# One tile's transpose moved from TensorE to the DMA engines, in an attention and FFN kernel whose TensorE order is a fixed list

## The chip, the cores and the metric

One core of one Trainium2 chip. The time is the device time of one launch in microseconds, as the median of several runs; "span" is the profiled execution from its first to its last instruction, about 1.7 us less. All positions are us from the start of the span. In the profile's lines PE is TensorE, PEld its weight loads, DVE VectorE, ACT ScalarE, POOL GpSimd and SP SyncE; SPq and ACTq are the instruction queues of SP and ACT, and L383 is line 383 of the kernel.

## The reference, cut to what matters

```python
# q, k, v: (4 batches, 8 heads, 768, 64); window 128 and 4 sink keys
scores = scale * q @ k.T                       # per head
a = softmax(where(sink | in_window, scores, -1e9))
x = (a @ v)  -> (4*768, 512)                   # heads side by side
out = ((x @ w1) * (x @ w2)) @ w3 @ w_out       # (3072, 512) float32
```

## The kernel before: the parts that matter

The kernel folds w3 and w_out into one matrix while the inputs load, then works through the batches. Of each batch b and each tile t of 256 rows: `sc` (scores of one pair of heads), exponential on ScalarE, mask multiply on VectorE, `av` (weighted values, then the division into `xn`), the transpose of `xn` into `xT`, gates `g` (x @ w1 copied by ScalarE, x @ w2 multiplied onto it by VectorE), and projections `p`. A task of TensorE's list is named after its kind and its place: `sc`, `av` and `xt` by batch, pair of heads and tile, `g` by batch, half of the rows, column block and which of the two matrices, `p` by batch and block of 128 rows. The transpose is done in one of two ways, by the list `X_XPOSE`:

```python
def x_transposes(b, r0, t):                    # on TensorE, through PSUM
    me = ("xt", b, r0, t)
    xt = ps_mm.tile([P, 2, 2, P], BF16, tag="mm", name="xt")
    for r in range(2):
        for i in range(2):
            nc.tensor.transpose(xt[:, r, i, :], xns[b, t][:, i, r0 + r, :, :]..., ident[:])
    yield
    copy_on(me, xT[b][:, r0:r0 + 2, t * 256:(t + 1) * 256], xt[:]...)
    yield

def x_transposes_dma(b, t, i):                 # 128 rows x 512, by DMA, issued on SP
    q0 = t * 256 + i * P
    nc.sync.dma_start_transpose(out=xT[b][:, :, q0:q0 + P], in_=xns[b, t][:, i]...)
    yield
```

The exponential and its multiply, whose buffers will matter (the pool's default is three):

```python
work = ctx.enter_context(tc.tile_pool(name="work", bufs=3))
...
ex = work.tile([P, 2, 512], BF16, tag="ex", name="ex")
nc.scalar.activation(ex[:, :, c0:], sc[:, :, c0:], ACTF.Exp, scale=scale)
yield
am = work.tile([P, 2, 512], BF16, tag="am", bufs=4, name="am")
nc.vector.tensor_mul(am[:, :, c0:], ex[:, :, c0:], mk)
```

TensorE's order is a list in the source (`PLAN`), found by a search. While the program is built, a small model of the engines runs through it and puts the instructions of ScalarE, VectorE and SP in the order in which they become ready by its own clock. It knows the landings (`arrive`, `LATER`), the latencies of DMA transposes (`XP_US`, `XX_US`), and, of the rings of buffers, these two in PSUM; a few buffers in SBUF it knows as dependencies (those of `xn`, for one), but the ring of `ex` not:

```python
rings = {n: [[0.0] for _ in range(k)] for n, k in (("mm", 4), ("sc", 2))}
...
queue[e].append((at + HOP, YIELD.get(k["name"][0], 0.1), us, k))
```

The softmax here doesn't subtract the row's maximum and nothing guards it: scores larger than these inputs give would overflow.

## Time and profile before

| | before |
|---|---|
| median of the runs | 196.68 us (4 runs, 196.50 to 196.72) |
| profiled span | 195.0 us |
| TensorE starts its unbroken work | 11.1 us |
| last TensorE piece starts | 190.16 us |
| x tiles transposed on TensorE / by DMA | 6 / 6 |

The profile's own lines are shown in the prediction. What to take from them: a chain made of TensorE alone, piece on piece, means that the time is a sum of TensorE's work. A change can then only save what it takes out of that sum, and can lose any amount by a wait.

### The profile page before, as it was taken

To read this page: it belongs to the slowest core of one execution; us is meant where nothing else is said; L and a number is where in the kernel's file an instruction comes from. 1 tells how busy PE (TensorE), PEld (TensorE's weight loads), DVE (VectorE), ACT (ScalarE), POOL (GpSimd) and SP (SyncE) were. 2 spreads that over 40 slices of the span, in tenths; PEclk is the share of its full clock that TensorE was granted. 3 is DMA by queue.
4 is the path that set the end of the run, shared out by engine and by line. 5 is a ranking of instruction groups with operands and counts; after the bars stand their busy time and mean duration, and the time that the engine had idled before them with its cause. 6 is when DMAs were issued, how large, how long until landed. Compare 5 with 4: busy or idle time off the path is not lost.

```text
span 195.0 us, 4886 instructions
## 1 busy us (share of the span) xinstructions
PE 188.8 (97%) x1986; PEld 127.8 (66%) x1986; DVE 119.5 (61%) x286; ACT 101.6 (52%) x181; POOL 74.0 (38%) x98
## 2 busy tenths in 40 slices
PE   7799999999999999999999999999999999999993
PEld 3689978889878766565665655566675565556543
DVE  5453878877787873687576857664677443323412
ACT  2223788896465666758266456464546533224210
POOL 7985657688999444355663500000000000000000
PEclk9999999999999999999999999999999999999999
DMA  6999999999999999999999999994122212131034
GB/s 223 242 188 189 175 177 193 193 178 157 154 155 138 183 116 206 191 176 178 141 155 122 155 168 149 226 195 63 27 30 54 111 55 54 53 110 55 0 122 147
DMA packets 103702, 27.32 MB, mean 140 GB/s; under 512 B 95232, under 2 KB 99712, under 8 KB 103680
## 3 DMA queue, kind: packets, MB, share of 16 engines
q0 software_dynamic: 77744, 13.90, 93.5%
q1 hardware_dynamic: 25792, 13.05, 35.2%
q8 instruction: 15, 0.25, 0.5%
q10 hardware_dynamic: 144, 0.07, 0.1%
q14 instruction: 7, 0.06, 0.1%
HBM read 29.36 MB, written 6.29 MB: 183 GB/s over the span
## 4 chain that ended last, share of the span: by engine, by line
PE 93%; DMA 4%; DVE 1%; POOL 0%; issue 0%; ACT 0%
PE pg L383 43%; PE po L423 20%; PE pw L413 8%; PE av L343 8%; PE sc L309 6%; DMA wo_sb<-in_moe_w_out_dram 4%; PE tp L261 2%; PE xt L360 1%; PE tp L233 1%; PE po L440 1%; PE sp L303 1%; PE tp L402 1%; PE vp L284 1%; DVE maskt L183 0%; POOL ident L190 0%
## 5 line engine op out<-in xcount | busy, mean ns | idle before, releaser
L383 PE MATMUL pg<-xT,w_sb 128*128 128x384 bf16 (+1 forms) x576 | 90.4, 308 | 0.0
L383 PEld LDWEIGHTS <-w_sb 128*128 128x128 bf16 x576 | 54.2, 98 | 27.7 <-issue 1.6
L387 DVE TENSOR_TENSOR ab<-a_sb,pg 128x384 bf16<-128x384 f32 (+1 forms) x72 | 36.5, 509 | 33.7 <-PE pg L383 30.4
L317 ACT ACTIVATE ex<-sc 128x1024 bf16<-128x1024 f32 (+1 forms) x48 | 44.7, 954 | 11.9 <-PE sc L309 9.4
L390 ACT COPY a_sb<-pg 128x384 f32<-128x384 f32 (+1 forms) x72 | 31.9, 445 | 36.5 <-PE pg L383 25.8
L423 PE MATMUL po<-w3o,ab 128*128 128x512 bf16 x184 | 42.5, 379 | 0.0
L321 DVE TENSOR_TENSOR am<-ex,maskt 128x1024 bf16<-128x1024 bf16 (+1 forms) x48 | 30.1, 641 | 3.1 <-ACT ex L317 2.9
L423 PEld LDWEIGHTS <-ab 128*128 128x128 bf16 x184 | 17.4, 98 | 18.9 <-issue 0.3
L350 DVE TENSOR_TENSOR xn<-av,rec 128x256 bf16<-128x256 f32 x48 | 20.4, 425 | 1.7
L115 POOL DMA_DIRECT2D vN<-in_v_dram x18 | 15.9, 884 | 12.1 <-DMA kN<-in_k_dram 8.5
L115 POOL DMA_DIRECT2D kN<-in_k_dram x18 | 15.9, 885 | 9.4 <-DMA qN<-in_q_dram 7.0
L343 PE MATMUL av<-vN,am 128*128 128x65 bf16 x352 | 18.6, 193 | 0.0
L226 ACT COPY o_sb<-po 128x512 f32<-128x512 f32 x14 | 8.2, 586 | 19.6 <-PE po L423 19.6
L343 PEld LDWEIGHTS <-am 128*128 128x128 bf16 x352 | 16.5, 97 | 2.0 <-issue 0.3
L115 POOL DMA_DIRECT2D qN<-in_q_dram x18 | 15.9, 886 | 4.9 <-DMA vN<-in_v_dram 3.6
L413 PE MATMUL pw<-wo_sb,w3t 128*128 128x128 bf16 x256 | 15.9, 219 | 0.4 <-DMA wo_sb<-in_moe_w_out_dram 0.4
L413 PEld LDWEIGHTS <-w3t 128*128 128x128 bf16 x256 | 14.4, 98 | 1.3 <-DMA wo_sb<-in_moe_w_out_dram 0.5
L309 PE MATMUL sc<-qT,kT 64*128 64x128 bf16 (+1 forms) x256 | 14.1, 238 | 0.0
L347 DVE RECIPROCAL rec<-av 128x4 f32<-128x4 f32 x48 | 8.5, 177 | 8.1 <-PE av L343 7.9
L226 DVE COPY o_sb<-po 128x512 f32<-128x512 f32 x9 | 6.2, 692 | 11.7 <-PE po L423 11.6
L343 PE MATMUL av<-vs,es 128*128 128x130 bf16 x64 | 12.3, 220 | 0.0
L309 PEld LDWEIGHTS <-kT 64*128 64x128 bf16 x256 | 8.2, 94 | 4.7 <-issue 3.2
(69 smaller groups left out, 125.0 us busy)
## 6 DMA issues: line engine op xcount, KB each, us to landing
out_dram<-o_sb SPq DMA_DIRECT2D x23, 256.0 KB, 5.1
vN<-in_v_dram POOLq DMA_DIRECT2D x24, 128.0 KB, 10.7
kN<-in_k_dram POOLq DMA_DIRECT2D x18, 128.0 KB, 11.8
qN<-in_q_dram POOLq DMA_DIRECT2D x18, 128.0 KB, 11.9
w_sb<-in_moe_w_dram POOLq DMA_DIRECT2D x8, 256.0 KB, 9.4
ab<-in_moe_w_dram SPq DMA_DIRECT2D x3, 512.0 KB, 4.0
ab<-in_moe_w_dram POOLq DMA_DIRECT2D x5, 256.0 KB, 9.5
wo_sb<-in_moe_w_out_dram POOLq DMA_DIRECT2D x4, 256.0 KB, 8.8
```

The costliest lines, as they stand in the source:

```text
L115: nc.gpsimd.dma_start(out=dst, in_=rows(src, b, kb))
L226: (nc.scalar.copy if home[me] == "act" else nc.vector.tensor_copy)(dst, src)
L309: nc.tensor.matmul(sc[:, e, c:c + n], kT[b][hp, r, kb * P:(kb + 1) * P], qT[b][hp, r, qb * P:qb * P + n], start=True, stop=True)
L317: nc.scalar.activation(ex[:, :, c0:], sc[:, :, c0:], ACTF.Exp, scale=scale)
L321: nc.vector.tensor_mul(am[:, :, c0:], ex[:, :, c0:], mk)
L343: nc.tensor.matmul(o, lhs, rhs, start=(n == 0), stop=(n == len(todo) - 1), skip_group_check=True)
L350: nc.vector.tensor_mul(xns[b, t][:, :, r, :, :], av[:, :, :, 0:D], rec[:].to_broadcast([P, 2, 2, D]))
L383: nc.tensor.matmul(pg[:], w_sb[:, kk, dt * P:(dt + 1) * P], xT[b][:, kk, tk], start=(kk == 0), stop=(kk == NP - 1))
L387: nc.vector.tensor_mul(ab[b][:, dt, tk], gate_a.pop((b, c, dt))[:], pg[:])
L390: nc.scalar.copy(a_sb[:], pg[:])
L413: nc.tensor.matmul(po[:], w3T[i][:, j, :], wo_sb[:, j, n0:n1], start=(j == 0), stop=(j == KFF - 1))
L423: nc.tensor.matmul(po[:], ab[b][:, kk, m * P:(m + 1) * P], w3o[:, kk, :], start=(kk == 0), stop=(kk == KFF - 1))
```

## The change

Batch 1's last tile (1, 2) joins the list of tiles transposed by DMA. That takes the two tasks `xt.1.0.2` and `xt.1.2.2` off TensorE. Since the result then lands some 8 us later, the whole order after the 100th task was searched anew, with the landing and latency tables set to what a trace with this transpose showed.

```diff
-    X_XPOSE = [(2, 0), (2, 1), (2, 2), (3, 0), (3, 1), (3, 2)]
+    X_XPOSE = [(1, 2), (2, 0), (2, 1), (2, 2), (3, 0), (3, 1), (3, 2)]
...
-    LATER = ((0.0,) * 6, (0.0,) * 6, (-4.0, -4.0, -2.0, 0.0, 1.0, 1.0), (3.0, 3.0, 3.0, 2.5, 3.5, 7.0))
+    LATER = ((0.0,) * 6, (0.0,) * 6, (-6.0, -4.0, -1.9, 0.2, 2.7, 2.4), (5.6, 5.8, 7.0, 8.4, 11.0, 11.5))
...
-    XP_US, XX_US, LATE_US = (0.0, 8.0, 8.3, 7.5), (9.0, 9.0, 9.0, 7.5, 7.5, 4.5, 3.5, 3.5, 3.5), 12.0
+    XP_US, XX_US, LATE_US = (0.0, 7.2, 6.9, 6.9), (7.0, 7.0, 7.0, 7.0, 7.5, 6.5, 2.7, 1.3, 1.3), 12.0
     PLAN = """
...
+        ... sc.2.2.0 sc.2.3.0 g.1.0.2.1 g.1.0.1.0 g.1.0.1.1 g.1.0.5.0 av.2.0.0
+        g.1.0.5.1 g.1.0.4.0 g.1.0.4.1 p.0.2 p.1.2 ...
```

(The list is cut; 337 tasks remain, the same ones but for the two.)

More of the change, by code (lines that the diff above doesn't have):

```diff
@@ L535 @@
         sc.0.3.2 g.0.0.0.1 g.0.1.6.0 g.0.1.7.0 g.0.1.7.1 g.0.1.0.0 g.0.1.0.1 g.0.1.6.1 g.0.0.5.0
-        g.0.0.4.0 g.0.0.5.1 av.0.0.2 g.0.1.3.0 g.0.0.4.1 tpk.1.0 g.0.1.4.0 tpq.1.0 g.0.1.2.0 av.0.1.2
-        av.0.2.2 g.0.1.2.1 sc.1.0.0 sc.1.1.0 g.0.1.3.1 g.0.1.5.0 sv.1 g.0.1.4.1 g.0.1.5.1 av.0.3.2
-        xt.0.0.2 sc.1.2.0 sc.1.3.0 tpq.1.1 tpk.1.1 xt.0.2.2 p.0.1 g.0.2.3.0 g.0.2.7.0 g.0.2.7.1
-        g.0.2.6.0 g.0.2.3.1 g.0.2.0.0 g.0.1.1.0 av.1.0.0 g.0.2.6.1 g.0.2.0.1 g.0.2.5.0 g.0.2.5.1
-        av.1.1.0 sc.1.0.1 sc.1.1.1 av.1.2.0 g.0.1.1.1 xt.1.0.0 g.0.2.2.0 g.0.2.2.1 p.0.2 av.1.3.0
@@ L541 @@
-        sc.1.2.1 sc.1.3.1 av.1.0.1 av.1.1.1 xt.1.2.0 p.0.0 xt.1.0.1 av.1.2.1 p.0.3 g.0.2.4.0 av.1.3.1
-        g.0.2.4.1 g.0.2.1.0 g.0.2.1.1 xt.1.2.1 sc.1.0.2 sc.1.1.2 p.0.4 g.1.0.4.0 g.1.0.3.0 sc.1.2.2
-        sc.1.3.2 g.1.0.0.0 av.1.0.2 av.1.1.2 p.0.5 xt.1.0.2 g.1.0.0.1 g.1.0.3.1 av.1.2.2 av.1.3.2
-        sc.2.0.0 sc.2.1.0 sv.2 g.1.0.4.1 g.1.0.6.0 xt.1.2.2 g.1.0.6.1 sc.2.2.0 sc.2.3.0 g.1.0.5.0
-        g.1.1.4.0 g.1.0.5.1 g.1.1.3.0 g.1.1.3.1 g.1.1.2.0 g.1.1.2.1 av.2.0.0 g.1.1.4.1 g.1.0.1.0
@@ L546 @@
-        g.1.1.1.0 g.1.1.1.1 g.1.0.1.1 g.1.0.2.0 g.1.0.2.1 av.2.1.0 av.2.2.0 av.2.3.0 sc.2.0.1 sc.2.1.1
-        g.1.1.5.0 g.1.1.5.1 g.1.0.7.0 g.1.1.6.0 sc.2.2.1 sc.2.3.1 g.1.0.7.1 g.1.1.7.0 g.1.1.6.1 p.1.0
-        g.1.1.0.0 g.1.1.0.1 av.2.0.1 av.2.1.1 av.2.2.1 av.2.3.1 sc.2.0.2 sc.2.1.2 g.1.1.7.1 p.1.1 p.1.4
-        sc.2.2.2 sc.2.3.2 av.2.0.2 av.2.1.2 p.1.2 sc.3.0.0 sc.3.1.0 sv.3 av.2.2.2 av.2.3.2 p.1.3
-        sc.3.2.0 sc.3.3.0 p.1.5 g.2.0.5.0 g.2.0.5.1 g.2.0.3.0 av.3.0.0 g.2.0.4.0 g.2.0.3.1 g.2.0.7.0
@@ L551 @@
-        g.2.0.7.1 g.2.0.2.0 av.3.1.0 sc.3.0.1 sc.3.1.1 g.2.0.2.1 g.2.0.4.1 g.2.0.6.0 g.2.0.6.1 g.2.1.0.0
-        g.2.1.0.1 g.2.1.3.0 g.2.1.3.1 g.2.1.2.0 g.2.1.6.0 g.2.1.6.1 g.2.0.1.0 g.2.0.1.1 av.3.2.0
-        av.3.3.0 sc.3.2.1 sc.3.3.1 g.2.1.2.1 g.2.1.4.0 g.2.0.0.0 g.2.1.4.1 g.2.0.0.1 g.2.1.1.0 g.2.1.1.1
-        g.2.1.7.0 av.3.0.1 g.2.1.7.1 av.3.1.1 av.3.2.1 av.3.3.1 sc.3.0.2 sc.3.1.2 g.2.1.5.0 g.2.1.5.1
-        p.2.1 sc.3.2.2 sc.3.3.2 av.3.0.2 av.3.1.2 p.2.0 p.2.4 g.3.0.7.0 g.3.0.7.1 g.3.0.6.0 g.3.0.6.1
@@ L556 @@
-        g.3.0.0.0 av.3.2.2 g.3.0.3.0 g.3.0.0.1 g.3.0.2.0 g.3.0.4.0 av.3.3.2 g.3.0.2.1 p.2.2 g.3.0.3.1
-        g.3.0.1.0 g.3.0.1.1 g.3.0.5.0 g.3.0.5.1 g.3.0.4.1 p.2.3 p.3.1 g.3.1.2.0 g.3.1.5.0 g.3.1.1.0
-        g.3.1.1.1 p.3.0 g.3.1.5.1 g.3.1.2.1 g.3.1.0.0 g.3.1.0.1 g.3.1.6.0 g.3.1.7.0 g.3.1.7.1 g.3.1.4.0
-        g.3.1.4.1 g.3.1.6.1 g.3.1.3.0 g.3.1.3.1 p.2.5 p.3.3 p.3.5 p.3.2 p.3.4
+        g.0.0.4.0 av.0.0.2 g.0.0.5.1 g.0.1.1.0 g.0.1.1.1 tpk.1.0 g.0.1.2.0 g.0.0.4.1 tpq.1.0 av.0.1.2
+        av.0.2.2 av.0.3.2 sc.1.0.0 sc.1.1.0 p.0.1 xt.0.0.2 xt.0.2.2 sc.1.2.0 sc.1.3.0 tpk.1.1 g.0.1.3.0
@@ new lines @@
+        g.0.2.0.0 g.0.2.0.1 g.0.1.3.1 g.0.1.2.1 g.0.2.5.0 g.0.2.5.1 g.0.2.2.0 sv.1 g.0.2.4.0 g.0.2.4.1
+        tpq.1.1 g.0.2.7.0 g.0.2.2.1 g.0.1.4.0 av.1.0.0 av.1.1.0 sc.1.0.1 sc.1.1.1 av.1.2.0 g.0.2.7.1
+        xt.1.0.0 p.0.0 av.1.3.0 g.0.1.4.1 sc.1.2.1 sc.1.3.1 xt.1.2.0 g.0.1.5.0 g.0.1.5.1 g.0.2.3.0
+        g.0.2.6.0 g.0.2.6.1 p.0.3 av.1.0.1 g.0.2.1.0 g.0.2.1.1 g.0.2.3.1 av.1.1.1 av.1.2.1 av.1.3.1
+        p.0.5 xt.1.0.1 sc.1.0.2 sc.1.1.2 xt.1.2.1 p.0.4 g.1.0.0.0 g.1.0.6.0 g.1.0.2.0 av.1.0.2 av.1.1.2
@@ new lines @@
+        sc.1.2.2 sc.1.3.2 g.1.0.6.1 g.1.0.0.1 g.1.0.7.0 g.1.0.3.0 sc.2.0.0 sc.2.1.0 sv.2 av.1.2.2
+        av.1.3.2 g.1.0.7.1 g.1.0.3.1 sc.2.2.0 sc.2.3.0 g.1.0.2.1 g.1.0.1.0 g.1.0.1.1 g.1.0.5.0 av.2.0.0
+        g.1.0.5.1 g.1.0.4.0 g.1.0.4.1 p.0.2 p.1.2 av.2.1.0 av.2.2.0 sc.2.0.1 sc.2.1.1 av.2.3.0 p.1.1
+        g.1.1.3.0 g.1.1.3.1 g.1.1.1.0 g.1.1.1.1 g.1.1.7.0 g.1.1.7.1 g.1.1.2.0 sc.2.2.1 sc.2.3.1
+        g.1.1.2.1 p.1.0 g.1.1.0.0 g.1.1.0.1 av.2.0.1 av.2.1.1 av.2.2.1 av.2.3.1 sc.2.0.2 sc.2.1.2
@@ new lines @@
+        g.1.1.4.0 g.1.1.5.0 g.1.1.5.1 g.1.1.4.1 g.1.1.6.0 g.1.1.6.1 sc.2.2.2 sc.2.3.2 av.2.0.2 p.1.3
+        av.2.1.2 av.2.2.2 sc.3.0.0 sc.3.1.0 p.1.5 sv.3 av.2.3.2 sc.3.2.0 sc.3.3.0 p.1.4 g.2.0.6.0
+        g.2.0.7.0 g.2.0.6.1 g.2.0.3.0 av.3.0.0 g.2.0.3.1 g.2.0.1.0 g.2.0.7.1 g.2.0.5.0 g.2.0.4.0
+        g.2.0.5.1 g.2.0.1.1 g.2.0.0.0 g.2.0.2.0 av.3.1.0 av.3.2.0 av.3.3.0 sc.3.0.1 sc.3.1.1 g.2.0.0.1
+        g.2.0.4.1 g.2.1.1.0 g.2.1.0.0 g.2.1.1.1 g.2.0.2.1 g.2.1.2.0 g.2.1.2.1 g.2.1.5.0 g.2.1.5.1 p.2.1
@@ new lines @@
+        sc.3.2.1 sc.3.3.1 g.2.1.0.1 g.2.1.4.0 g.2.1.4.1 g.2.1.3.0 g.2.1.3.1 g.2.1.7.0 g.2.1.7.1 av.3.0.1
+        av.3.1.1 av.3.2.1 av.3.3.1 sc.3.0.2 sc.3.1.2 g.2.1.6.0 p.2.2 av.3.0.2 sc.3.2.2 sc.3.3.2
+        g.2.1.6.1 p.2.0 g.3.0.4.0 g.3.0.7.0 av.3.1.2 av.3.2.2 av.3.3.2 g.3.0.6.0 g.3.0.6.1 p.2.3
+        g.3.0.4.1 g.3.0.2.0 g.3.0.2.1 p.2.5 g.3.0.7.1 g.3.1.6.0 g.3.1.0.0 g.3.1.3.0 g.3.1.6.1 g.3.1.2.0
+        g.3.1.2.1 g.3.1.0.1 g.3.1.5.0 g.3.1.5.1 g.3.1.3.1 g.3.1.7.0 g.3.1.1.0 g.3.1.1.1 g.3.0.5.0
@@ L560 @@
+        g.3.0.5.1 g.3.1.7.1 g.3.0.0.0 g.3.0.0.1 g.3.0.3.0 g.3.0.3.1 g.3.0.1.0 g.3.0.1.1 g.3.1.4.0
+        g.3.1.4.1 p.3.2 p.3.4 p.3.0 p.3.3 p.3.1 p.2.4 p.3.5
     """
```

## The prediction

> **What bounds the kernel now.** I read the page first, then the chain that ended last in order of time, then the groups of TensorE by line, then the tiles xn and xT. From the page:
>
> ```profile
> span 195.0 us, 4886 instructions
> ...
> PE 188.8 (97%) x1986; PEld 127.8 (66%) x1986; DVE 119.5 (61%) x286; ACT 101.6 (52%) x181; POOL 74.0 (38%) x98
> ...
> PE   7799999999999999999999999999999999999993
> ...
> PEclk9999999999999999999999999999999999999999
> DMA  6999999999999999999999999994122212131034
> ...
> PE 93%; DMA 4%; DVE 1%; POOL 0%; issue 0%; ACT 0%
> ```
>
> TensorE is busy in every slice but the first and the last, at full granted clock, and 93% of the chain is TensorE itself. The DMA engines are full up to about 135 us and then nearly free: a transfer moved into the first stretch meets a queue, one in the second does not. Busy TensorE is not proof that nothing waits, so the chain in order of time comes next (start, length, what, number of instructions):
>
> ```profile
> 3.12 7.96 DMA wo_sb<-in_moe_w_out_dram
> 11.08 0.05 issue
> 11.12 5.21 PE pw L413 x88
> ...
> 80.34 0.76 PE pg L383 x4
> ...
> 83.53 0.22 PE xt L360 x4
> ...
> 87.83 0.22 PE xt L360 x4
> 88.05 0.65 PE pg L383 x4
> ...
> 190.16 1.78 PE po L440 x24
> 191.94 0.02 issue
> 191.96 0.27 ACT o_sb L446
> ```
>
> The reader is to see that after the first weights land at 11.1 us every piece is TensorE and each starts where the one before ended, up to 191.94: no wait lies on TensorE's path for 181 us. So the time is 11.1 us of start, the sum of TensorE's pieces, and 3.1 us of evacuation and last store. Only three things can change it: less TensorE work, another price for the same work, or a wait that the new order lets in. The two xt pieces at 83.53 and 87.83 are the ones at issue. Last, the tile xT:
>
> ```profile
> L370 SPq DMA_TRANSPOSE xT<-xn x12: 1189/1258/2657, 100.9 to 163.3; - x12
> L226 ACT COPY xT<-xt x11: 586/586/592, 28.0 to 88.2; 128x512 bf16<-128x512 bf16 x11
> ...
> DMA to landing us min/median/max: 2.3/5.1/8.6
> ```
>
> Twelve DMA transposes of x are in use already (min/median/max of their issue in ns); the TensorE ones are evacuated by ScalarE at 586 ns.
>
> **What the Trainium skill says.** "TensorE: Matmul & The Clock Gate", section "Back-to-back issue gap", gives N/2.4 + 2.5 ns for a warm matmul, 56 ns at N=128. The trace agrees: 0.223 us from one four-transpose piece to the next, 56 ns each. So the group's mean of 219 ns for L360 is a latency and must not be multiplied by eight. "TensorEngine Tiling (Array Packing)", section "Key Properties", says that a change of tiling mode drains the array. The trace agrees: a four-matmul gate piece takes 0.65 us, but 0.76 at 80.34, next to row-tiled scores; over all pieces the median price is 0.096 us. "VectorE: DVE Perf Modes", section "The three transpose paths", has 1309 ns for a 128x128 DMA transpose; this case's ones, 128x512 each, take 2.3 to 8.6 us to land, so I use those. "DMA: Bandwidth & Descriptors", section "Issuing engines are not separate DMA queues", says that all DMAs share 16 engines whoever issues them. The trace fits: 8.1 to 8.6 us to landing for x transposes issued at 100 to 115 us, 2.3 to 2.4 for those after 145 us.
>
> **The change, part by part.** (1) Removed: the tasks xt of batch 1, tile 2: two groups of four transposes. On TensorE 2 x 0.22 = 0.45 us, all on the path. On ScalarE two copies, 2 x 0.586 = 1.2 us, off the path, since ScalarE is 52% busy. Two uses of the four-buffer PSUM ring go as well. (2) Added: two DMA transposes, 2 x 1.26 = 2.5 us of SP issue, nothing on TensorE; their price is latency and queue time. (3) Moved: from the 101st entry the whole TensorE order is another one. I counted both lists: the same 337 tasks otherwise, and 59 changes of tiling mode in each, so the order itself neither saves nor costs drains. (4) The tables of expected landings and latencies are only the scheduler's beliefs; they set the order on SP and the other queues and cost nothing by themselves. (5) The last task is again a projection in three pieces with the same store order (the count that selects it moves from 2 to 4 modulo 8, both the default), so the tail stays.
>
> Without a new wait: 195.0 - 0.45 = 194.55 us of span. The timed run is 1.7 us over the span (196.69 against 195.0), which gives 196.25 us.
>
> **Where a wait could come in.** I re-priced the new list with the trace's median durations (gate piece 0.650 at 384 columns and 0.437 at 256, projection 1.727, values 0.357, one scores task 0.231, a mode change 0.096), starting at the last common task, 46.6 us. That is an estimate of when TensorE would reach each task if it never waits. Against it I set the landings of the trace before:
> - x of batch 1, tile 2: the last values task starts at 85.3. In the trace the like case (batch 2, tile 0) took 11.8 us from there (98.7) to the second landing (110.5). So about 97.1; first needed by a gate at 98.6. Slack 1.5 us.
> - The last q block of batch 2: landed at 100.3 (issued 92.9, 7.4 us). The diff itself moves the expected arrival of that block by +1.4 us, and by up to 3.2 if the 0.9 us per added transpose in its queue model comes on top: 101.7 to 103.5, needed at 103.25. Slack 1.6 to -0.2.
> - q and k of batch 3, tile 0: landed at 114.0; moved by 2.8 to 4.6 on the same reading: 116.8 to 118.6, needed at 117.3. Slack 0.5 to -1.3.
> - x of batch 2, tile 1: values end as before (108.9 against 109.2) and it took 13.8 us to the second landing at 123.0: about 122.7. But the gates of batch 2 now begin at 122.3 instead of 130.4. Slack -0.4.
> - x of batch 2, tile 2, by the same reckoning (12.6 us): 132.3, needed at 133.4. Slack 1.1.
> Such waits do not add up: once TensorE has waited 0.4 us, all later needs are 0.4 us later too. The largest deficit counts: between 0 and 1.3 us. I take 0.3 as the middle, because the words say that the order was searched on landings from a trace with this transpose in it, so my too-late cases are probably those where SP now issues earlier. Span 194.85, time about 196.5 us.
>
> **The rivals.** (a) *The saving comes through whole*, 196.2: for it speaks that the kernel before, ordered in the same manner, has no wait at all after 11 us. Against it, the old order had 7 us of slack at the gates of batch 2 and the new one has none. (b) *A landing takes the place of the saved work*: two more transposes enter the full DMA stretch, the loads behind them slip, and TensorE stands before a score or a gate of batch 2 or 3. That gives 196.7 to 197.6. (c) *Another engine or the PSUM ring becomes the bound*: DVE is at 61% and ScalarE at 52%, but the order bunches gates, whose evacuation costs 0.51 us on DVE and 0.45 on ScalarE per 0.65 of TensorE. Gates ran back to back for 8.6 us in the old order without a wait, so I expect nothing here. (d) *The transposes are hidden and a slipped arrival spreads*: several waits on input that shift each other, 2 to 4 us, if the arrival tables are wrong for this order. Possible, since a fixed order cannot step aside, but unlikely.
>
> **Range and chances.** Nothing in the change can save more than 0.45 us, so faster by 2% (3.9 us) is practically out. The low end is the full saving and a little noise (the three runs before spread 0.2 us): 196.0. The high end is the worst of the deficits above plus some: 197.7. Slower by over 2% needs rival (d).
>
> **What would show it.** Right: 40 TensorE transposes at L360 instead of 48, 14 DMA transposes of xT, nine or ten ScalarE copies into xT, TensorE's chain again unbroken from 11 us, its last piece ending near 191.5 instead of 191.94. The first two new transposes, issued near 87 us, should take about 8 us to land. Rival (b) would show as an idle gap of TensorE before a score near 103 or 117 us or a gate near 122 us, with a DMA transpose as releaser. The prediction would be wrong if the loads of batch 3 slip by more than 5 us, if the SP queue holds a transpose of x behind one that still waits for its input, or if gaps on TensorE sum to over 1.5 us.

## The result, and the profile after

196.51 us (4 runs, 196.39 to 196.63) against 196.68: ratio 0.9993, 95% interval 0.9976 to 1.0011. A ratio here is the mean time of one kernel's fast runs over that of the other's in the same rounds, so not quite the quotient of the medians. The change is the same in speed; the forecast of 196.5 was met. But the trace shows that it was met by another wait than the forecast named.

The page of the changed kernel, cut to the lines that answer to those of before (and one group of part 5: busy us, mean ns of one, idle us before and what ended it):

```profile
span 194.9 us, 4859 instructions
...
PE 187.6 (96%) x1965; PEld 127.4 (65%) x1978; DVE 119.0 (61%) x285; ACT 101.2 (52%) x180; POOL 73.8 (38%) x98
...
L383 PE MATMUL pg<-xT,w_sb 128*128 128x384 bf16 (+1 forms) x576 | 89.2, 308 | 0.3 <-ACT a_sb L390 0.3
...
L423 PE MATMUL po<-w3o,ab 128*128 128x512 bf16 x171 | 41.7, 379 | 0.7
```

The gates' matmuls (L383) had 0.0 us of idle time before them in the old kernel; now 0.3, ended by ScalarE's copy of a gate. The 0.7 at the projections is no wait: this trace lacks 13 records of that line (171 of 184; the weight loads, which are complete, number 184), and each missing one leaves a gap of 0.05 us. A reader who takes every gap for a wait is misled here.

The tile xT: 14 DMA transposes in place of 12, ten copies out of PSUM in place of twelve (four of them now on VectorE, where before it was one), and the two new transposes in their window:

```profile
L370 SPq DMA_TRANSPOSE xT<-xn x14: 1190/1257/1966, 87.1 to 159.2; - x14
L226 ACT COPY xT<-xt x6: 585/586/592, 28.1 to 63.9; 128x512 bf16<-128x512 bf16 x6
L226 DVE COPY xT<-xt x4: 425/425/425, 54.5 to 76.8; 128x512 bf16<-128x512 bf16 x4
...
L370 SPq DMA_TRANSPOSE xT<-xn x2: 1190/1226/1261, 87.1 to 88.3; - x2
...
DMA to landing us min/median/max: 7.2/7.8/8.4
```

They were issued at 87.1 and 88.3 and landed by 96.7 at the latest (88.3 + 8.4); the first gate that reads them ran at 99.1. That transfer is hidden. I then laid the new list against the trace, each task at the median price it has in the trace of before. In the whole stretch from 46 us to the last gate one single task came late by more than 0.04 us: a gate at 90.81, late by 0.42. The chain of waits around it (start, length, what):

```profile
87.67 0.77 PE pg L383 x4
88.44 0.02 issue
88.46 0.56 DVE ab L387
89.01 0.48 DVE am L321
89.49 0.02 issue
89.51 0.02 ACTq L317
89.53 0.04 issue
89.58 0.81 ACT ex L317
90.39 0.38 ACT a_sb L390
90.77 0.04 issue
90.81 2.11 PE pg L383 x12
```

For 2.4 us the chain leaves TensorE and runs through VectorE and ScalarE: a mask multiply (am), an exponential (ex), a copy of a gate (a_sb), and only then a gate on TensorE. TensorE works on meanwhile and loses only the last 0.42 us; the page's idle of 0.3 is less, since the ends of matmuls are modelled and run on into the gap. (At another place, from 62.99 to 74.04, the chain of the changed kernel's page leaves TensorE for a DMA transpose of q; there no task of TensorE was late, so that stretch is no wait.) The timeline of the two engines there tells why (start, length, engine, line; in brackets the idle time before it and what ended it):

```profile
84.87 1.52 ACT L317 ACTIVATE ex<-sc 128x768 bf16<-128x768 f32 x2
...
87.54 0.81 ACT L317 ACTIVATE ex<-sc 128x768 bf16<-128x768 f32 x1 [1.15 <-PE sc L309]
...
88.46 0.56 DVE L387 TENSOR_TENSOR ab<-a_sb,pg 128x384 bf16<-128x384 f32 x1 [0.49 <-PE pg L383]
88.93 0.55 DVE L321 TENSOR_TENSOR am<-ex,maskt 128x768 bf16<-128x768 bf16 x1
...
89.58 0.81 ACT L317 ACTIVATE ex<-sc 128x768 bf16<-128x768 f32 x1 [1.23 <-DVE am L321]
...
90.28 0.86 ACT L390 COPY a_sb<-pg 128x384 f32<-128x384 f32 x2
...
90.81 1.95 PE L383 MATMUL pg<-xT,w_sb 128*128 128x384 bf16 x11 [0.25 <-ACT a_sb L390]
```

Three exponentials of batch 2 are done by 88.4. The fourth takes the buffer of the first, and the first is read by a multiply that VectorE has in its order behind a gate product. That product waits for a gate on TensorE until 88.46; VectorE idles 0.49 us although the multiply could have run since 85.7. So ScalarE idles 1.23 us, the two gate copies queue behind the exponential, and the gate that takes the PSUM buffer of the first of them, four buffers on in the ring, waits on TensorE.

### The profile page after: what moved, and what is told of

The parts are those of the page before. It is cut to its first block, busy times and chain, and to the rows that moved or that the text cites. A ratio compares the mean times of both kernels' runs of the same rounds, so it can differ in the third digit from the quotient of the medians.

```text
span 194.9 us, 4859 instructions
## 1 busy us (share of the span) xinstructions
PE 187.6 (96%) x1965; PEld 127.4 (65%) x1978; DVE 119.0 (61%) x285; ACT 101.2 (52%) x180; POOL 73.8 (38%) x98
## 4 chain that ended last, share of the span: by engine, by line
PE 86%; DMA 8%; SPq 2%; DVE 1%; ACT 1%; issue 1%; ACTq 0%
PE pg L383 40%; PE po L423 18%; PE pw L413 7%; PE av L343 7%; PE sc L309 6%; DMA qT<-qN 4%; DMA ab<-in_moe_w_dram 4%; PE tp L261 2%; SPq L270 1%; PE tp L402 1%; PE xt L360 1%; PE tp L233 1%; PE po L440 1%; PE sp L303 1%; DVE w3t L226 1%
## 5 line engine op out<-in xcount | busy, mean ns | idle before, releaser
L383 PE MATMUL pg<-xT,w_sb 128*128 128x384 bf16 (+1 forms) x576 | 89.2, 308 | 0.3 <-ACT a_sb L390 0.3
L383 PEld LDWEIGHTS <-w_sb 128*128 128x128 bf16 x576 | 54.6, 98 | 27.9 <-issue 1.4
L423 PE MATMUL po<-w3o,ab 128*128 128x512 bf16 x171 | 41.7, 379 | 0.7
L226 ACT COPY o_sb<-po 128x512 f32<-128x512 f32 x18 | 10.5, 586 | 24.9 <-PE po L423 24.9
L343 PE MATMUL av<-vN,am 128*128 128x65 bf16 x352 | 18.1, 193 | 0.0
L309 PE MATMUL sc<-qT,kT 64*128 64x128 bf16 (+1 forms) x256 | 14.1, 238 | 0.0
L226 DVE COPY o_sb<-po 128x512 f32<-128x512 f32 x5 | 3.5, 692 | 9.6 <-PE po L423 9.6
```

The lines of the kernel that those rows point to most:

```text
L226: (nc.scalar.copy if home[me] == "act" else nc.vector.tensor_copy)(dst, src)
L309: nc.tensor.matmul(sc[:, e, c:c + n], kT[b][hp, r, kb * P:(kb + 1) * P], qT[b][hp, r, qb * P:qb * P + n], start=True, stop=True)
L343: nc.tensor.matmul(o, lhs, rhs, start=(n == 0), stop=(n == len(todo) - 1), skip_group_check=True)
L383: nc.tensor.matmul(pg[:], w_sb[:, kk, dt * P:(dt + 1) * P], xT[b][:, kk, tk], start=(kk == 0), stop=(kk == NP - 1))
L423: nc.tensor.matmul(po[:], ab[b][:, kk, m * P:(m + 1) * P], w3o[:, kk, :], start=(kk == 0), stop=(kk == KFF - 1))
```

## The experiments

Theory A: the saving of 0.45 us was lost to this ring of three exponential buffers, which the scheduler's model leaves out, as its code shows. Rival B: the gates come too close together for the evacuations or for the four PSUM buffers. Rival C: a landing. Twelve runs were made, on three chips, two of them of the unaltered kernels; all gave right results. TensorE's waits are read off each profiled run as above: tasks late by 0.1 us or more after 30 us, against the prices of the trace of before.

| run | median, us (lowest to highest, runs) | span | TensorE's waits in the profile |
|---|---|---|---|
| first call: before beside it | 198.08 (196.46 to 199.24, 11) | | |
| e1_after_ex4 | 196.63 (196.07 to 197.52, 6) | 195.8 | 0.75 at the scores, 104.7 |
| e2_am_early | 196.58 (196.18 to 196.87, 6) | 194.5 | none |
| e3_before_ex4 | 196.65 (196.48 to 197.94, 6) | 194.9 | none |
| e4_dma_only | 205.85 (205.10 to 208.20, 5; the highest counted as slow) | 206.5 | 7.06 at a gate, 98.7 |
| second call: before beside it | 196.68 (196.41 to 197.11, 11) | | |
| e5_order_only | 196.74 (196.67 to 197.18, 5) | 195.2 | none |
| e6_after_again | 196.67 (196.41 to 196.87, 5) | 194.9 | 0.42 at a gate, 90.8 |
| e7_am_ex4 | 196.73 (196.14 to 197.43, 6) | 195.1 | 0.69 at the scores, 104.0 |
| e8_before_again | 196.83 (196.47 to 198.11, 6) | 194.9 | none |
| third calls: before beside them | 196.67 (196.41 to 200.28, 12; the highest counted as slow) | | |
| e9_score_later | 197.10 (196.86 to 199.19, 6) | 197.5 | 0.72 at the values, 112.0 |
| e10_score_much_later | 196.72 (196.55 to 197.13, 5) | 195.1 | 0.57 at the values, 110.3 |
| e11_am_again | 196.44 (196.29 to 197.01, 6) | 194.8 | 0.15 at the scores, 103.7 |
| e12_both_later | 196.50 (196.31 to 198.92, 6) | 194.7 | 0.11 at a gate, 49.1; 0.32 at a gate, 109.9 |

**A fourth buffer (e1).**

```diff
-        ex = work.tile([P, 2, 512], BF16, tag="ex", name="ex")
+        ex = work.tile([P, 2, 512], BF16, tag="ex", bufs=4, name="ex")
```

> The changed kernel with four buffers for the exponentials' tile in place of three, nothing else. Theory A (the tile's ring: ScalarE's fourth exponential waits for VectorE to have read the first, and the gate evacuations stand behind it): the one wait of TensorE near 90.8 us (0.42 us) goes, the last TensorE piece ends near 191.5 instead of 191.96, span about 194.5, time about 196.1 us, ratio to before 0.997. Rival B (the gates come too close together for the evacuations or the four PSUM buffers): a wait of 0.25 us or more stays near 90 us, time 196.5. Rival C (landings): unchanged, 196.5.

The wait near 90 us is gone, as A has it and B does not. In the traces TensorE, ScalarE and VectorE have all their instructions in the same order as in the changed kernel, so the fourth buffer is the only difference, and it is this ring that made the wait. The expected time did not come: in the profiled run another wait took its place at the scores of batch 2 that read the last transposed q block. The chain there:

```profile
95.38 9.27 DMA qT<-qN
104.64 0.04 issue
104.69 0.40 PE sp L303 x4
```

Issued at 95.38, landed 9.27 us later (this profiled run began 0.6 us late). In the changed kernel the same transpose was issued at 94.6 and took 8.0. This is the second item in the prediction's list, "needed at 103.25". So rival C is real too, but one place further on. The best of the six runs, 196.07, is what A had foretold; the median is not.

**VectorE's order alone (e2, and again e11).** The multiply is put ahead of the three gate products, by giving it the first place in its queue; three buffers as before. TensorE's and SP's orders do not change at all; on VectorE a few more neighbours move, and ScalarE trades one evacuation with it.

```diff
-            queue[e].append((at + HOP, YIELD.get(k["name"][0], 0.1), us, k))
+            early = e == "dve" and k["name"] == ("sc", 2, 0, 0)
+            queue[e].append((at + HOP, 0.0 if early else YIELD.get(k["name"][0], 0.1), us, k))
```

> The changed kernel with VectorE's multiply of the first exponential of batch 2 put ahead of the three gate products that it stood behind; three buffers as before. TensorE's and SP's order are untouched. Theory A: the exponential that waited can start at once, TensorE's wait near 90.8 us falls from 0.42 to under 0.1 us, time about 196.1 us. Rival B: the wait stays, or moves onto a gate product that is now later by 0.5 us; time 196.5.

The chain of e2 at the same place:

```profile
87.63 2.71 PE pg L383 x16
90.34 0.18 PE av L343 x6
90.52 1.95 PE pg L383 x12
...
103.41 0.33 PE sp L303 x4
```

Four gate pieces, the values, and the next gates without a break. The evacuating work was the same and the PSUM buffers were the same four, so B falls: ScalarE and VectorE had time enough, in another order. The span is 194.5 us, to the tenth what the prediction gave for no wait at all, and its last TensorE piece starts at 189.74 in place of 190.16 in the trace of before.

> The early multiply alone once more, on the chip of these runs, for the spread: theory says either no wait (span 194.5, time 196.2) or the q block's landing wait of up to 0.75 us (time up to 196.9), so a wider spread than the kernel before has.

In e11 the scores waited 0.15 us for the q block. Over the twelve runs of e2 and e11 the median is 196.56, between 196.18 and 197.01. The nine runs of the changed kernel (the four of the result and e6) have 196.58, between 196.39 and 196.87. The remedy lowers the best runs by 0.2 us and leaves the middle where it was.

**The control (e3).** The kernel before with four buffers.

> Control: the kernel before with four buffers for the exponentials. Its TensorE has no wait after 11 us, so theory A expects no gain: span 195.0, time 196.7 within 0.1 us. If a fourth buffer helps by itself (more than 0.2 us here too), then what e1 shows is not the removal of that one wait.

Span 194.9, no wait of TensorE, 196.65: no gain, as expected. The first call's chip ran the kernel before at 196.5 to 199.2 us, so its ratio of 0.9927 for e1 says nothing of the change: e3, the same order with a spare buffer, has 0.9941. What such runs are shows in the profile of e9, taken in a run of 199.19: the first w3 load in its chain landed at 10.38 us (issued at 1.73, 8.65 us), in the changed kernel's profile at 9.17, and the tasks of the folding stood 2.2 us later by 19 us. The late load is 1.2 us of that; the rest goes with the clock, which was granted at 0.50 from 10.7 to 14.1 us. In the three calls every run from 198.8 to 199.3 us has a mean granted clock of 0.991, and every run under 198.2 us one of 0.997 or more. It is a late start, before anything that the change touches.

**The DMA transposes without the new order (e4).** `X_XPOSE` as after, the old list without the two TensorE tasks, the old tables.

> The DMA transposes of batch 1's last tile in the old TensorE order (the two TensorE tasks taken out of the list, nothing else moved, old tables). Expected from the traces: TensorE reaches the first gate of that tile at 91.0 - 0.45 = 90.6 us, the second transpose lands at 96.7 to 97.1, so it waits about 6 us and the time is about 196.7 - 0.45 + 6 = 202.3 us. The rival, that the latency is hidden anyway and the new order is not needed, expects 196.25 us.

```profile
89.95 0.21 SPq L370
90.16 0.05 issue
90.21 8.34 DMA xT<-xn
98.55 0.14 issue
98.68 6.64 PE pg L383 x24
```

The gate waits 7 us for the landing and not 6. The first gate of the old list that reads this tile is the one that starts at 89.73 us in the trace of before; the expectation had taken a later one, at 91.0. So the latency is not hidden by itself; the new order is what the change needs. But the four fast runs (205.10 to 205.89) stand 8.9 us over the 196.68 of before, not 5.6, because of what the last line shows: 24 matmuls, six pieces of 0.65 us or 3.9 in all, took 6.64. The clock had gone down (us, busy time of PE, PEld, DVE, ACT and POOL, granted clock, packet time of the DMA engines over the stretch, GB/s):

```profile
60.00:90.00 30.00, 29.79 (x326) 20.66 (x329) 20.95 (x55) 18.91 (x33) 16.32 (x20) 1.00 1.95 169
90.00:98.00 8.00, 1.80 (x16) 0.73 (x14) 3.21 (x7) 2.48 (x4) 3.74 (x5) 0.73 1.86 160
98.00:105.00 7.00, 6.32 (x23) 3.08 (x24) 1.11 (x2) 1.25 (x3) 3.50 (x4) 0.57 1.75 156
```

After the idle time the mean granted clock is 0.57 for the next 7 us; in finer windows it is 0.50 from 93.8 to 103.9 and 1.00 on both sides. A wait of 7 us on TensorE thus cost 9.6: 7.06 and, by the same pricing, 2.6 for the slow gates. Less the 0.45 saved that is 9.2. (The profiled run is the one counted as slow: it began 2.3 us late as well, which is left out of this sum.)

**The new order without the DMA transposes (e5).** List and tables as after, the two TensorE tasks put back ahead of `sc.2.2.0`.

> The new TensorE order and tables, but batch 1's last tile transposed on TensorE again (its two tasks put in after the gates that follow the last values of batch 1). Expected: 0.45 us more TensorE work than the changed kernel; a wait near 90 us stays if it comes from the order and not from the DMA transposes (span about 195.3, time about 196.9), and goes if the transposes caused it (span 194.95, 196.55). For the loads: the last load of v of batch 3 landed at 126.8 us before and at 130.3 after; if the two extra transposes in the full DMA stretch did that, it lands near 127 here; if the new order did, near 130.

No wait near 90 us here, though TensorE's order is the new one but for these two tasks. In this build VectorE has the multiply at 87.97 already, ahead of the gate product that it waited behind, and the wait is absent. By the letter of what I expected, that would make the transposes the cause. But the trace of the changed kernel shows no wait on one, and e2 removes the wait with both transposes in place. What makes the wait is neither TensorE's list as such nor the transposes, but how the other engines' orders fell out around them; the two tasks put back also give ScalarE and VectorE 0.45 us more before that point, and this run cannot part the two. For the loads the run is clearer: the last load of v landed at 127.16 us; with the two transposes it landed at 130.25 (after) and 132.31 (e6), and before at 126.75 and 124.71 (e8). All nine profiles with the new order and both transposes have it at 130.25 to 132.42, all four without them (before, e3, e5, e8) at 124.71 to 127.16. That the transposes alone do it is still not shown: in e4, which has them in the old order, the last load landed at 120.92, though there TensorE's wait of 7 us held other transfers back as well.

**The change again, and both remedies (e6, e7, e8).**

> The changed kernel unaltered, on the same chip as the other runs of this call, since the chip of the first call gave the kernel before 196.5 to 199.2 us. Expected: TensorE's wait of about 0.4 us near 90.8 us again; time 196.5; ratio to before 0.999.

The same wait, 0.42 us at 90.82; 196.67 us, ratio 0.9997. It is a property of the program, not of one run.

> Both remedies at once: the early multiply and four buffers for the exponentials. Theory A: they remove the same wait, so nothing more than with one: span 194.5, time 196.15 on a quiet run, 0.4 us under the changed kernel. If the two add up (193.9 or less), they removed two different waits and the theory is incomplete.

No sum of gains, as A says: the ring's wait is gone once, and the landing's wait of 0.69 us at the scores is there. Since e7 stands at 195.1, or 194.4 without that wait, and not at 193.9 or less, the two remedies did not remove two different waits.

> The kernel before as a run of its own, to learn what the 199 us runs of the first call were. If they come from where a run stands in the round, this copy shows as few of them as the others (196.6 to 197); if the old order is less robust, it shows about half at 199. Expected: the former, 196.7 us.

196.83 us, one run at 198.11, none near 199, and none in the 11 runs beside it: the old order as such does not make the 199 us runs. They came on the first call's chip (5 of 11 runs of before) and singly on the third's (e9 199.19, e12 198.92), in old and new order.

**A version that beats both (e9, e10, e12).** With both remedies in, the scores that met the late q block were moved back in the list, behind a gate product (e9), behind a whole projection (e10, with the last two values tasks a gate later), and, in e12, as in e9 with the last two values tasks a gate later.

```diff
-        g.1.1.2.0 sc.2.2.1 sc.2.3.1 g.1.1.2.1 p.1.0 g.1.1.0.0 g.1.1.0.1 av.2.0.1 av.2.1.1 av.2.2.1 av.2.3.1 sc.2.0.2 sc.2.1.2 g.1.1.4.0 g.1.1.5.0
+        g.1.1.2.0 g.1.1.2.1 sc.2.2.1 sc.2.3.1 p.1.0 g.1.1.0.0 g.1.1.0.1 av.2.0.1 av.2.1.1 g.1.1.4.0 av.2.2.1 g.1.1.5.0 av.2.3.1 sc.2.0.2 sc.2.1.2   (e12)
```

> Both remedies of the ring, and the scores of batch 2 that need the last transposed q block moved behind one gate product (0.65 us later). In the traces with the ring's wait gone, TensorE waited 0.69 and 0.75 us for that block in two of three profiles. Expected if that landing is the next limit: this wait falls to about 0.1 us or none, median near 196.2 us, 0.4 to 0.5 us under the kernel before, and fewer runs near 197. If the wait comes again somewhere else (the gates of batch 2 near 122 us), the saving stays inside the noise.

> As e9, but those scores behind a whole projection (1.73 us later) and the two last values tasks of that tile behind one more gate. Expected: no wait at the scores at all; but x of batch 2, tile 1 is issued one or two transposes later on SP, so the gates of batch 2 at 122.3 us may now stand up to 1 us. If not, 196.2 us.

> Both remedies of the ring, the scores behind one gate product (as in e9), and the last two values tasks of that tile one gate later each, because in e9 and e10 TensorE waited 0.57 to 0.72 us before the last of them for its mask multiply. Expected: neither the landing wait at the scores nor the wait at the values; TensorE without a wait over 0.15 us, span 194.5, median near 196.2 us, ratio to before 0.9975. If a wait of a few tenths comes up at a third place, the saving of 0.45 us cannot be had by moving single tasks, and the time stays within 0.2 us of the kernel before.

In all three the wait at the scores is gone, and a new one has come: 0.72 and 0.57 us at the last values task, which waits there for its mask multiply, and in e12 0.32 us at a gate a little after. e9 and e10 are no faster than the kernel before (ratios 1.0039 and 1.0006), e12 has 196.50 with the ratio 1.0017, between 0.9977 and 1.0056. No version was found that beats both kernels beyond the spread; the nearest is the early multiply, at 0.9995 in the quiet call (0.9981 to 1.0008).

## Why the prediction was right, and where its reasoning failed

- **The bound and the saving held.** TensorE's sum is the time, and 0.45 us left it: where nothing waited (e2) the span was 194.5, the forecast's 194.55. "Without a new wait" was the right frame, and so was the offset of 1.7 us to the timed run.
- **The wait held in size and failed in kind.** The forecast put 0.3 us, "the largest deficit" of five landings. Measured were 0.42 us, at none of the five. All five landed in time in the changed kernel. The step that failed is rival (c): "Gates ran back to back for 8.6 us in the old order without a wait, so I expect nothing here." That argument is about the capacity of the evacuating engines, and capacity was indeed enough (e2); the prices there, 0.51 and 0.45 us, fall due once per two gate pieces, 1.30 us of TensorE, and not per 0.65. It says nothing of their order and of rings that are not PSUM. The 196.5 met the measurement by luck: one wait of 0.42 stood in for another of 0.3.
- **The landings, one by one.** The x transposes of batch 1: expected about 97.1, landed by 96.7. The last q block of batch 2: expected 101.7 to 103.5, landed near 102.7 (issued 94.6, 8.0 us), and in e1 at 104.6: an item with a slack of 1.6 to -0.2 that is a wait in some runs and none in others. In e6 it landed at 103.66, with the scores at 103.79: there it is hidden only because the ring's wait moves TensorE's need back by 0.42. Batch 3's q and k, tile 0: expected 116.8 to 118.6, landed by 115.6, needed at 117.9. Batch 2's x, tile 1: I expected 122.7, a deficit of 0.4, by carrying over the 13.8 us of the old trace. Its second transpose was issued at 112.8 and took at most 8.4: 121.2 at the latest, needed at 122.9. Carrying over a delay that contains SP's old queue was one mistake; the prediction said itself that this could be so. Two more lie in its reading of the old trace. The gates of batch 2 began there at 122.87 us, not at 130.4 (that is where the old list has the task with which the new list begins), so the "7 us of slack" of rival (a) was not there. And that gate at 122.87 ran before the second transpose had landed at 123.01: these gates read the first 384 rows, of which that transpose holds none. The first transpose landed at 121.33 in the old trace (slack 1.5) and at 119.8 in the new (slack 3.1). Batch 2's x, tile 2: expected 132.3, landed at 130.6, needed at 134.0.
- **That waits do not add up but the largest counts** is what e1, e7 and e9 to e12 show: where the foremost wait was taken away, the next came up with 0.15 to 0.75 us, and only e2's profile has none. What held the other runs of e2 and e11 near 196.6 is not shown, since one run of each was profiled.
- **What was to be seen:** 14 DMA transposes, and the first two at 7.2 and 8.4 us to landing, as said. Nine or ten ScalarE copies were wrong (six, and four on VectorE), without effect. "TensorE's chain again unbroken" was wrong, and its last piece started at 190.18, ending near 191.96 and not near 191.5. One of its signs of being wrong came up and meant nothing: two loads of k of batch 3 landed 5.2 and 5.6 us later than in the trace of before (in e6 up to 7.6), and no task of TensorE waited for them.
- **A citation.** The Trainium skill, "TensorE: Matmul & The Clock Gate", section "Back-to-back issue gap", calls the formula that the prediction quotes the gap of an isolated matmul, and has about 81 ns at N=128 for a stream of weight loads and matmuls. The trace decides for the prediction's 56 ns.

## What to carry to other kernels

Where one engine's chain is unbroken, price a change as "work taken out, less the largest new wait", and look for that wait in every ring of buffers, also those between two engines that are not the bound: a free ScalarE and VectorE can still stop TensorE by the order of their queues. A small saving from a list that is packed to the tenth of a microsecond is soon taken up by the next constraint, and removing one wait then shows in the trace but, as here, not in the median. When a model orders the queues, put every ring with few buffers into it.

## What the Trainium skill lacked or had wrong

- "TensorE: Matmul & The Clock Gate", Part 1, gives a warm-up of about 3.4 us of sustained work after an idle window of as long, and calls the window free-running. In e4 the clock was at 0.50 for about 10.2 us, which is three such windows. After the restart at 98.7 us the gates ran at about double price (1.28 us in place of 0.65) to about 103.8 us, so some 5.1 us; that is longer than 3.4, but fits a restart in the middle of a window. The drop came 1.9 us after the modelled end of the last matmul (91.8 to 93.7), earlier than an idle window of 3.4 us would have it. It is one gap in one run.
- "VectorE: DVE Perf Modes", "The three transpose paths", gives one figure for a DMA transpose and none for one beside loads. Here 128x512 transposes took 2.3 us to land with the DMA engines free and up to 9.8 us with them full (a kT in e1). By how much two more of them put the other loads off stays open: the last load landed 3.1 to 7.7 us later in the nine profiles with them and the new order than in the four without, but not in e4.
